# Splitting one opening load over two hardware queues and re-ordering the first quarter of a fused attention and SwiGLU kernel

## The chip, the cores and the metric

The kernel runs on one core of a Trainium2 chip. The metric is device microseconds (us) of that core; the median of five runs of the kernel before is 332.36 us (331.88 to 332.77). The core's engines are PE (TensorE, matrix products into eight PSUM banks), DVE (VectorE), ACT (ScalarE), POOL (GpSimd) and SP (SyncE). Each takes its own instructions strictly in program order. POOL here does nothing but issue loads; SP issues the transposes done by DMA and the stores.

## The reference

Causal sliding-window attention, window 64, over 8 batches of 8 heads of 576 tokens with 64 channels, and then a gated feed-forward block (FFN) on the 4608 tokens:

```python
scores = (1/8) * q @ k.T;  allowed where 0 <= i - j < 64
attn = softmax(scores);  x = attn @ v           # [4608, 512] over all heads
g = x @ w_gate;  val = x @ w_val                # [4608, 1536]
out = (g * sigmoid(g) * val) @ w_out            # [4608, 512]
```

All inputs and the output are float32 in memory; the matrix products run in bfloat16.

## The kernel before

**Tiles.** Attention works on 36 blocks of 128 tokens (n = 0 to 35). The FFN works on nine chunks of 512 tokens, four blocks each, and on twelve pieces f of 128 hidden channels. Tokens cross batches at 4.5 blocks, so blocks 4 and 13 (and others) need two loads for each of q, k and v.

**Two regimes.** The opening covers the attention of blocks 0 to 13 and FFN chunks 0 and 1. It is written out by hand as two strings of short words, `LOADS` (L162) and `STEPS` (L166), which `build` (L675) reads word by word; each word appends its operations to the engines' queues in that order. After it a regular loop (from L717) runs the FFN of chunks 2 to 8, with the second FFN product of the chunk before and the attention of the blocks ahead between its pieces. `_Graph` (L31) derives the semaphore waits from what each operation reads and writes.

**The words of `LOADS`.** Each issues DMAs, nearly all from POOL's queue: `q:n`, `kq:n`, `v:n` load a block (`kq` is two DMAs, q first, 128 KB in bfloat16 each), `w:a:b` loads pieces a to b-1 of w_gate and then of w_val (two DMAs), `wo:a:b` loads pieces of w_out in one DMA. `ld:n` in `STEPS` loads q, k and v of block n. `f:0` is `first_load` (L285): k of block 0 in float32, in two halves of 64 partitions, which are not cast by the DMA but by the words `ca` and `cd`. `init` builds the identity and the masks on DVE.

**The words of `STEPS`.** `warm:a:b` is a products of b columns that nobody reads, and `W:a` is a such products of 512 columns. `TQ:n`, `TK:n` transpose q and k on PE (4 instructions into one bank); `qa`, `ka` evict the result on ACT and `qd`, `kd` on DVE. `T:0:h` with `ea`/`ed` does the same for the first k. `TD:n` transposes k and q by two DMAs on SP's queue. `S:n` is the 24 score products and two exponentials on ACT; `M:n` masks the result on DVE (two operations). A block that had `B:n` before its scores has the mask added by two PE products of 512 columns and needs no `M`. `A0:n` and `A1:n` are the two phases of the product with v (16 instructions each; the second waits for the end of the first), `N:n` is its normalisation on DVE (four operations). `X:n` transposes the result on PE, evicted by `xa` or `xd`; `XD:n` does it with a DMA. `F:c:f:t0:t1` is piece f of FFN chunk c for the token columns t0 to t1 (0 to 512 if not given): four products with w_gate, the tanh on ACT, four products with w_val. `U` does the two DVE operations (L611, L613) of the oldest `F` that has not had its own yet, and frees its two banks. `O:c:u` is the product with w_out for 128 tokens: 12 products of 512 columns and a store.

**What orders it.** An operation that needs a bank takes the one freed longest ago in program order and waits until it has been emptied, so PE can run ahead of DVE only by the banks that are left. An `F` over columns t0 to t1 waits only for the blocks of x in that range. The first `F` of the kernel before, `F:0:7:0:256`, needs blocks 0 and 1 and stands behind `X:2`.

Of the kernel before, what the change touches and what calls it, by code (L numbers as in the profile page):

```python
# [7 lines left out]
B, H, S, D = 8, 8, 576, 64  # L8
DM, DFF = H * D, 1536
T = B * S  # L10
# [139 lines left out]
class _Kernel:  # L150
# [9 lines left out]
    LAST = NFC  # L160
    NI = 1
    LOADS = """  # L162
    f:0 init q:0 kq:1 kq:2 v:1 v:0 kq:3 v:2 v:3 w:7:9 w:1:2 w:5:6 kq:4 kq:5 w:3:4 w:4:5 w:6:7 v:5 w:2:3 v:6
    v:4 w:9:10 w:0:1 kq:6 v:7 kq:7 w:10:12
    """
    STEPS = """  # L166
    warm:45:64 B:0 B:1 ca:0:0 cd:0:1 T:0:1 T:0:0 ea:0:1 TQ:0 ld:8 wo:0:6 ed:0:0 qa:0 W:1 TQ:1 S:0 qd:1 TK:1
    ld:9 kd:1 W:1 TQ:2 S:1 qd:2 TK:2 kd:2 W:2 S:2 W:1 A0:0 A0:1 A1:0 A1:1 ld:10 N:0 TQ:3 B:3 qa:3 N:1 TK:3 X:0
    ka:3 xa:0 M:2 W:1 S:3 X:1 A0:2 xd:1 A1:2 ld:11 N:2 W:1 A0:3 A1:3 N:3 W:1 X:2 F:0:7:0:256 xd:2 U X:3
    F:0:8:0:384 xd:3 F:0:1 U U F:0:5 U TK:4 TQ:4 ld:12 ka:4 TQ:5 F:0:7:256:512 qd:4 TK:5 qa:5 F:0:8:384:512 U  # L170
    S:4 U F:0:3 kd:5 M:4 S:5 U F:0:4 M:5 U F:0:6 U F:0:2 U A0:4 A0:5 A1:4 ld:13 wo:6:12 A1:5 F:0:9 N:4 N:5 X:4
    F:0:0 U xa:4 X:5 U TK:6 xa:5 TQ:6 ld:14 F:1:0:0:128 ka:6 U F:1:1:0:256 qa:6 TQ:7 U F:1:2:0:256 qd:7 S:6
    TK:7 U F:1:3:0:256 kd:7 F:0:10 M:6 U U A0:6 S:7 A1:6 ld:15 TQ:8 TK:8 N:6 F:0:11 M:7 ka:8 qd:8 X:6 A0:7
    xa:6 S:8 U A1:7 ld:16 F:1:4:0:384 N:7 F:1:5:0:384 U X:7 U TQ:9 xa:7 F:1:6:0:384 M:8 qa:9 TK:9 U F:1:7 kd:9
    TD:10 U A0:8 S:9 A1:8 ld:17 F:1:8 N:8 M:9 X:8 TQ:11 xa:8 F:1:9 U qd:11 A0:9 TK:11 U A1:9 ka:11 F:1:10 N:9
    TK:12 U X:9 ka:12 TQ:12 F:1:11 xd:9 qd:12 TD:13 S:10 U S:12 F:1:0:128:512 M:10 F:1:1:256:512 M:12 A0:10 U
    S:11 A1:10 U F:1:2:256:512 F:1:3:256:512 N:10 F:1:4:384:512 U XD:10 F:1:5:384:512 O:0:0 U U U M:11 O:0:1
    A0:11 S:13 A1:11 O:0:2 N:11 M:13 X:11 O:0:3 xd:11 F:1:6:384:512 U TD:14 TD:15
    """

    def __init__(self, nc, q, k, v, wg, wv, wo, out):
# [103 lines left out]
    def first_load(self, n):  # L285
        (_, b, s, L), = self.segs(128 * n, 128)
        for u in range(2):
            d = self.ff[n][64 * u:64 * u + 64].rearrange("p h j d -> p h (j d)")
            a = self.k[b, 4 * u:4 * u + 4, s:s + L, :].rearrange("h (p j) d -> p h (j d)", j=2)
            self.g.op("sp", lambda e, d=d, a=a: e.dma_start(d, a), writes=[("ff", n, u)], dma=True)  # L290

    def cast(self, n, half, eng):
        hs = slice(2 * half, 2 * half + 2)
# [489 lines left out]
```

The softmax here doesn't subtract the row's maximum and nothing guards it: scores larger than these inputs give would overflow.

## Time and profile before

| what | value |
|---|---|
| median of five runs | 332.36 us (331.88 to 332.77) |
| the profiled execution, its own time | 332.36 us, of it 330.2 us span |
| first `F` begins on PE | 17.55 us |
| first `O` begins on PE | 71.48 us |
| regular loop begins (`F` of chunk 2) | 83.27 us |
| POOL busy issuing loads | without a pause from 1.25 to about 68 us |
| DMA engines | 9 tenths or more in each slice up to about 200 us |

Times in the profile are counted from the start of the span. A row of the timeline gives start and length, the engine, the line, what was written from what, and how many instructions were merged; a length includes the time to drain, so the distance between starts is what an instruction occupies its engine. "POOLq", "SPq" and "ACTq" are the queues on which DMAs are issued; "to landing" is counted from the start of the issue. The granted TensorE clock is 1.00 throughout in this profile.

### The profile page before, as it was taken

Reading aid. Unit: us, or ns where it says so; the run is one execution under the profiler, and the core shown is the slowest. Engines: PE = TensorE matmul, PEld = TensorE weight load, DVE = VectorE, ACT = ScalarE, POOL = GpSimd, SP = SyncE. Lnnn points to the kernel's source line nnn. Section 1 sums busy time; section 2 is a strip of 40 time slices with the busy share of each in tenths; the row PEclk is TensorE's granted clock in tenths of the full one; section 3 lists DMA queues with packets and bytes.
Section 4 is the critical chain, followed back from the end, with each engine's and each line's share of the span. In section 5 each row is a group of like instructions: output and inputs, shape, how many; then the busy total and the mean of one; then the engine's idle time right before and its main releaser. Section 6 shows DMA issues by size and latency. Waiting matters only on the chain.

```text
span 330.2 us, 8380 instructions
## 1 busy us (share of the span) xinstructions
PE 324.8 (98%) x3543; PEld 166.3 (50%) x3543; DVE 216.7 (66%) x457; ACT 136.0 (41%) x247; POOL 116.5 (35%) x145
## 2 busy tenths in 40 slices
PE   7999999999999999999999999999999999999996
PEld 5565665564455444444445454545454544444444
DVE  5689999992467748585757676767676766555520
ACT  3736566453344334343525252525343432332222
POOL 8999999957017506060706060100000000000000
PEclk9999999999999999999999999999999999999999
DMA  9999999999999999999999999542424111100012
GB/s 102 168 169 172 154 183 155 158 144 185 185 172 137 165 179 75 181 85 172 85 173 82 174 70 189 66 112 36 126 35 128 34 64 34 64 34 32 32 64 98
DMA packets 169366, 38.56 MB, mean 117 GB/s; under 512 B 160369, under 2 KB 164849, under 8 KB 169329
## 3 DMA queue, kind: packets, MB, share of 16 engines
q0 software_dynamic: 123600, 18.75, 86.3%
q1 hardware_dynamic: 45584, 19.21, 29.3%
q8 instruction: 28, 0.46, 0.6%
q14 instruction: 10, 0.07, 0.1%
q10 hardware_dynamic: 144, 0.07, 0.1%
HBM read 37.75 MB, written 9.44 MB: 143 GB/s over the span
## 4 chain that ended last, share of the span: by engine, by line
PE 93%; DVE 3%; DMA 2%; SPq 0%; issue 0%
PE ps L602 55%; PE ps L635 27%; PE ps L421 3%; DMA xT<-xb 2%; PE ps L534 2%; PE ps L309 2%; PE ps L471 2%; PE ps L665 1%; PE ps L568 1%; PE ps L401 1%; PE ps L357 1%; DVE xb L493 1%; DVE xb L556 0%; SPq L584 0%; DVE mask L267 0%
## 5 line engine op out<-in xcount | busy, mean ns | idle before, releaser
L611 DVE SCALAR_TENSOR_TENSOR uu<-sig,ps 128x512 bf16<-128x512 bf16 (+3 forms) x117 | 75.2, 643 | 66.5 <-ACT sig L608 66.2
L602 PE MATMUL ps<-xT,Wg 128*128 128x512 bf16 (+3 forms) x468 | 112.5, 363 | 0.4 <-DMA xT<-xb 0.4
L602 PE MATMUL ps<-xT,Wv 128*128 128x512 bf16 (+3 forms) x468 | 112.5, 363 | 0.0
L608 ACT ACTIVATE sig<-ps 128x512 bf16<-128x512 f32 (+3 forms) x117 | 66.0, 565 | 89.3 <-PE ps L602 89.2
L635 PE MATMUL ps<-Wo,hT 128*128 128x512 bf16 x420 | 97.8, 379 | 0.0
L613 DVE SCALAR_TENSOR_TENSOR hT<-uu,ps 128x512 bf16<-128x512 bf16 (+3 forms) x117 | 75.5, 645 | 4.0
L371 POOL DMA_DIRECT2D va<-in_v_dram x40 | 39.5, 1021 | 87.9 <-PE ps L534 86.6
L602 PEld LDWEIGHTS ps<-xT,Wv 128*128 128x128 bf16 x468 | 45.0, 98 | 48.9 <-DVE hT L613 0.5
L602 PEld LDWEIGHTS ps<-xT,Wg 128*128 128x128 bf16 x468 | 43.8, 98 | 46.5 <-DMA xT<-xb 1.1
L635 PEld LDWEIGHTS ps<-Wo,hT 128*128 128x128 bf16 x420 | 39.9, 98 | 46.6
L431 ACT ACTIVATE pt<-ps 128x512 bf16<-128x512 f32 x72 | 37.8, 600 | 26.8 <-PE ps L421 26.7
L647 ACT ACTIVATE ost<-ps 128x512 f32<-128x512 f32 x35 | 20.9, 597 | 66.1 <-PE ps L635 66.0
L283 POOL DMA_DIRECT2D qn<-in_q_dram x40 | 40.5, 1032 | 3.2 <-issue 2.4
L283 POOL DMA_DIRECT2D kn<-in_k_dram x39 | 39.7, 1041 | 1.4 <-DMA kn<-in_k_dram 1.3
L437 DVE TENSOR_TENSOR pt<-pt,mask 128x512 bf16<-128x512 bf16 x66 | 24.3, 417 | 0.2
L556 DVE TENSOR_TENSOR xb<-ps,rp 128x448 bf16<-128x448 f32 (+1 forms) x36 | 18.5, 514 | 1.2
L553 DVE RECIPROCAL rp<-ps 128x7 f32<-128x7 f32 (+1 forms) x36 | 6.7, 187 | 15.5 <-PE ps L534 15.5
L421 PE MATMUL ps<-qT,kT 64*64 64x64 bf16 (+1 forms) x864 | 16.0, 205 | 0.2
L421 PEld LDWEIGHTS ps<-qT,kT 64*64 64x64 bf16 x864 | 12.4, 109 | 7.2 <-DVE hT L613 4.2
L534 PE MATMUL ps<-va,pt 64*64 64x65 bf16 x728 | 11.5, 193 | 0.1
L493 DVE TENSOR_TENSOR xb<-ps,rc 128x256 bf16<-128x256 f32 x24 | 10.2, 424 | 0.8
L377 POOL DMA_DIRECT2D Wv<-in_moe_w_val_dram x10 | 9.7, 969 | 0.0
(50 smaller groups left out, 104.9 us busy)
## 6 DMA issues: line engine op xcount, KB each, us to landing
out_dram<-ost SPq DMA_DIRECT2D x35, 256.0 KB, 2.5
qn<-in_q_dram POOLq DMA_DIRECT2D x32, 128.0 KB, 7.6
va<-in_v_dram POOLq DMA_DIRECT2D x32, 128.0 KB, 6.7
kn<-in_k_dram POOLq DMA_DIRECT2D x31, 128.0 KB, 7.9
Wo<-in_moe_w_out_dram POOLq DMA_DIRECT2D x2, 768.0 KB, 12.2
Wg<-in_moe_w_gate_dram POOLq DMA_DIRECT2D x8, 128.0 KB, 5.4
Wv<-in_moe_w_val_dram POOLq DMA_DIRECT2D x8, 128.0 KB, 5.3
Wg<-in_moe_w_gate_dram POOLq DMA_DIRECT2D x2, 256.0 KB, 5.6
```

The costliest lines, as they stand in the source:

```text
L283: self.g.op("pool", lambda e, d=d, a=a: e.dma_start(d, a), writes=ks, dma=True)
L371: g.op("pool", lambda e, d=d, a=a: e.dma_start(d, a), writes=ks, dma=True)
L421: r = e.matmul(sv[h][o:o + 64, c, q0:q1], self.kT[ps, c, kk:kk + 64], qT[ps, c, q0:q1], start=not biased, stop=not biased or c == 3 and kk ...
L431: g.op("act", lambda e, po=po, si=si: e.activation(po, si, ACTF.Exp, scale=SCALE), reads=[bk], writes=[pk])
L437: "dve", lambda e: e.tensor_tensor(po, po, m, ALU.mult), reads=[pk, "mask"], writes=[pk]))
L556: g.op("dve", lambda e, xo=xo, rb=rb, a=a: e.tensor_tensor(xo, a[:, :, 0:64], rb, ALU.mult), reads=[bk] + rk, writes=wk)
L602: r = e.matmul(bank[:, 0:n], W[:, kk, f * 128:f * 128 + 128], xT[:, kk, t0:t1], start=(kk == 0), stop=(kk == NK - 1))
L608: g.op("act", lambda e: e.activation(sig[:, 0:n], G[:, 0:n], ACTF.Tanh, scale=0.5), reads=[gk], writes=[("sig", i)])
L611: g.op("dve", lambda e: e.scalar_tensor_tensor(uu[:, 0:n], sig[:, 0:n], 1.0, G[:, 0:n], ALU.add, ALU.mult), reads=[("sig", i), gk], writes ...
L613: g.op("dve", lambda e: e.scalar_tensor_tensor(hT[:, f, t0:t1], uu[:, 0:n], 0.5, V[:, 0:n], ALU.mult, ALU.mult), reads=[("uu", i), vk], wr ...
L635: r = e.matmul(OB[:, :], hT[:, f, 128 * u:128 * u + 128], self.Wo[:, f, :], start=(f == 0), stop=(f == NF - 1))
L647: g.op("act", lambda e: e.activation(ost[:, :], OB[:, :], ACTF.Copy), reads=[ok], writes=[("ost", io)])
```

## The change

The two halves of k of block 0 are issued from SP and from ACT, one each, instead of both from SP. The order of loads and of steps in the opening is replaced as a whole. Names that differ: the warm-up is 50 products of 86 columns; `B:1` stands behind `TQ:0`; v of block 0 is loaded ahead of v of block 1; the first weights are pieces 2, 3 and then 0, 1, in 256 KB DMAs; the weights come in 16 DMAs instead of 20; both halves of w_out are loaded behind block 12; the first `F` is `F:0:2:0:128`, behind `X:1`, and pieces 2, 3, 0 and 1 of chunk 0 are cut in the token direction, as are pieces 0 to 4 of chunk 1 (128 and 384 columns). Block 4 gets `B:4` and loses `M:4`; `X:5` becomes `XD:5`; blocks 12 and 13 change places between `TD` and PE transposes. The loop is not touched.

```diff
     LOADS = """
-    f:0 init q:0 kq:1 kq:2 v:1 v:0 kq:3 v:2 v:3 w:7:9 w:1:2 w:5:6 kq:4 kq:5 w:3:4 w:4:5 w:6:7 v:5 w:2:3 v:6
-    v:4 w:9:10 w:0:1 kq:6 v:7 kq:7 w:10:12
+    f:0 init q:0 kq:1 kq:2 v:0 kq:3 v:1 v:2 w:2:4 v:3 w:0:2 kq:4 kq:5 kq:7 kq:6 w:5:6 w:6:7 w:7:9 v:6 v:4
+    w:9:10 v:7 v:5 w:4:5 w:10:12
     """
     STEPS = """
-    warm:45:64 B:0 B:1 ca:0:0 cd:0:1 T:0:1 T:0:0 ea:0:1 TQ:0 ld:8 wo:0:6 ed:0:0 qa:0 W:1 TQ:1 S:0 qd:1 TK:1
-    ld:9 kd:1 W:1 TQ:2 S:1 qd:2 TK:2 kd:2 W:2 S:2 W:1 A0:0 A0:1 A1:0 A1:1 ld:10 N:0 TQ:3 B:3 qa:3 N:1 TK:3 X:0
-    ka:3 xa:0 M:2 W:1 S:3 X:1 A0:2 xd:1 A1:2 ld:11 N:2 W:1 A0:3 A1:3 N:3 W:1 X:2 F:0:7:0:256 xd:2 U X:3
-    F:0:8:0:384 xd:3 F:0:1 U U F:0:5 U TK:4 TQ:4 ld:12 ka:4 TQ:5 F:0:7:256:512 qd:4 TK:5 qa:5 F:0:8:384:512 U
-    S:4 U F:0:3 kd:5 M:4 S:5 U F:0:4 M:5 U F:0:6 U F:0:2 U A0:4 A0:5 A1:4 ld:13 wo:6:12 A1:5 F:0:9 N:4 N:5 X:4
-    F:0:0 U xa:4 X:5 U TK:6 xa:5 TQ:6 ld:14 F:1:0:0:128 ka:6 U F:1:1:0:256 qa:6 TQ:7 U F:1:2:0:256 qd:7 S:6
-    TK:7 U F:1:3:0:256 kd:7 F:0:10 M:6 U U A0:6 S:7 A1:6 ld:15 TQ:8 TK:8 N:6 F:0:11 M:7 ka:8 qd:8 X:6 A0:7
-    xa:6 S:8 U A1:7 ld:16 F:1:4:0:384 N:7 F:1:5:0:384 U X:7 U TQ:9 xa:7 F:1:6:0:384 M:8 qa:9 TK:9 U F:1:7 kd:9
-    TD:10 U A0:8 S:9 A1:8 ld:17 F:1:8 N:8 M:9 X:8 TQ:11 xa:8 F:1:9 U qd:11 A0:9 TK:11 U A1:9 ka:11 F:1:10 N:9
-    TK:12 U X:9 ka:12 TQ:12 F:1:11 xd:9 qd:12 TD:13 S:10 U S:12 F:1:0:128:512 M:10 F:1:1:256:512 M:12 A0:10 U
-    S:11 A1:10 U F:1:2:256:512 F:1:3:256:512 N:10 F:1:4:384:512 U XD:10 F:1:5:384:512 O:0:0 U U U M:11 O:0:1
-    A0:11 S:13 A1:11 O:0:2 N:11 M:13 X:11 O:0:3 xd:11 F:1:6:384:512 U TD:14 TD:15
+    warm:50:86 B:0 ca:0:0 cd:0:1 T:0:0 T:0:1 ea:0:0 ed:0:1 TQ:0 ld:8 B:1 qa:0 TQ:1 S:0 qd:1 TK:1 ld:9 kd:1 W:1
+    TQ:2 S:1 qd:2 TK:2 kd:2 W:1 A0:0 S:2 A1:0 N:0 TQ:3 B:3 qa:3 M:2 W:1 X:0 xa:0 TK:3 ka:3 W:1 A0:1 W:1 S:3
+    A1:1 ld:10 N:1 A0:2 A1:2 ld:11 N:2 W:2 X:1 F:0:2:0:128 xa:1 U X:2 F:0:3:0:256 xd:2 A0:3 U A1:3
+    F:0:2:128:384 N:3 F:0:0:0:384 U X:3 U TQ:4 xa:3 F:0:1:0:384 qd:4 TK:4 ld:12 wo:6:12 wo:0:6 U TQ:5 ka:4
+    F:0:3:256:512 qd:5 TK:5 F:0:0:384:512 U TQ:7 ka:5 F:0:1:384:512 U F:0:2:384:512 U TK:7 qa:7 S:5 U B:4 kd:7
+    S:4 TQ:6 TK:6 M:5 kd:6 F:0:5 qd:6 U S:6 S:7 F:0:6 M:6 F:0:7 M:7 U F:0:8 U U A0:4 A1:4 ld:13 F:0:9 N:4 U
+    A0:5 A0:6 A0:7 A1:5 ld:14 A1:6 ld:15 A1:7 X:4 N:5 xa:4 F:0:4 N:6 XD:5 F:0:10 N:7 U X:6 X:7 xa:6 F:0:11 U
+    xa:7 U TQ:8 TK:8 ld:16 qa:8 F:1:0:0:128 F:1:1:0:128 U F:1:2:0:128 F:1:3:0:128 U TQ:9 U ka:8 F:1:4:0:128 U
+    TK:9 qa:9 S:8 U F:1:5 kd:9 M:8 U A0:8 TD:10 S:9 A1:8 ld:17 F:1:6 N:8 M:9 X:8 TQ:11 xa:8 F:1:7 U qd:11 A0:9
+    A1:9 U F:1:8 N:9 TK:11 F:1:9 U TD:12 kd:11 X:9 F:1:10 U xd:9 F:1:11 U U F:1:0:128:512 S:10 U F:1:1:128:512
+    M:10 F:1:2:128:512 U A0:10 U S:11 A1:10 F:1:3:128:512 N:10 F:1:4:128:512 U XD:10 M:11 O:0:0 U A0:11 S:12
+    A1:11 TK:13 N:11 TQ:13 O:0:1 M:12 kd:13 qd:13 X:11 S:13 xd:11 O:0:2 M:13 O:0:3 TD:14 TD:15
     """
...
     def first_load(self, n):
...
-            self.g.op("sp", lambda e, d=d, a=a: e.dma_start(d, a), writes=[("ff", n, u)], dma=True)
+            self.g.op(("sp", "act")[u], lambda e, d=d, a=a: e.dma_start(d, a), writes=[("ff", n, u)], dma=True)
```

## The prediction

> **What bounds the kernel now.** First the page's busy shares and its chain:
>
> ```profile
> PE 324.8 (98%) x3543; PEld 166.3 (50%) x3543; DVE 216.7 (66%) x457; ACT 136.0 (41%) x247; POOL 116.5 (35%) x145
> ...
> PE 93%; DVE 3%; DMA 2%; SPq 0%; issue 0%
> ```
>
> PE sets the end. Only the opening is touched, so I next read busy time by stretch (length, then PE, PEld, DVE, ACT, POOL with instruction counts):
>
> ```profile
> 17.30:71.50 54.20, 54.12 (x778) 33.32 (x778) 49.34 (x117) 31.26 (x63) 52.59 (x65) 1.00 2.01 163
> 71.50:83.05 11.55, 11.55 (x116) 5.66 (x114) 4.97 (x16) 3.05 (x7) 6.99 (x8) 1.00 1.99 174
> ```
>
> From the first `F` PE is full, with DVE close behind (91%). What the change can win lies before 17.55, or in less PE work and fewer small gaps behind it. Then the timeline of the first stage, with the chain through it:
>
> ```profile
> 1.02 2.58 PE L345 MATMUL ps<-wz 128*128 128x64 bf16 x45 [1.02 <-DVE wz L255]
> 4.33 1.89 PE L401 MATMUL ps<-nmask,ident 128*128 128x512 bf16 x4 [0.73 <-DVE nmask L268]
> 5.69 0.42 ACT L299 ACTIVATE cc<-ff 128x256 bf16<-128x256 f32 x1 [3.46 <-DMA ff<-in_k_dram]
> 6.45 0.63 PE L309 MATMUL ps<-ident,qn 128*128 128x128 bf16 x4
> 7.87 0.64 PE L421 MATMUL ps<-qT,kT 64*64 64x128 bf16 x24
> 9.56 0.44 PE L421 MATMUL ps<-qT,kT 64*64 64x128 bf16 x24
> 11.55 0.86 PE L471 MATMUL ps<-va,pt 64*64 64x65 bf16 x56
> 12.30 0.18 DVE L490 RECIPROCAL rc<-ps 128x4 f32<-128x4 f32 x1 [1.50 <-PE ps L471]
> 17.55 0.60 PE L602 MATMUL ps<-xT,Wg 128*128 128x256 bf16 x4
> 20.05 1.03 PE L602 MATMUL ps<-xT,Wg 128*128 128x512 bf16 x4
> ```
>
> The reader sees k cast at 5.69, q transposed at 6.45, first scores at 7.87, first product with v at 11.55 (held by v), normalisation from 12.30, FFN from 17.55. Last, POOL and its landings, one issue at a time:
>
> ```profile
> 5.74 1.78 POOL L371 DMA_DIRECT2D va<-in_v_dram  x2
> ...
> 10.93 0.84 POOL L377 DMA_DIRECT2D Wg<-in_moe_w_gate_dram  x1
> ...
> va<-in_v_dram POOLq DMA_DIRECT2D x1, 128.0 KB, 4.7
> Wv<-in_moe_w_val_dram POOLq DMA_DIRECT2D x1, 256.0 KB, 5.7
> ```
>
> A load of q, k or v takes POOL 0.87 us and lands 4.7 to 5.0 us after its start (5.5 around 18 to 25); weights take 0.73 and land after 5.1 to 6.8.
>
> **k in halves.** Both came from SP: starts 0.73 and 1.53, landing 2.8 and 4.1 later, at 3.5 and 5.6. From ACT the second starts at about 0.74 and lands between 3.5 and 4.8, so casts (0.42) end by 5.2. But `B:0` comes first on PE: 45 products of 64 columns took 2.58 less 0.18 of drain, 53 ns each; 50 of 86 take 72 ns each, to 4.60, and two mask products at the 0.43 between the L401 starts end at 5.46. Transposes of k start there instead of at 6.04. The next step, `TQ:0`, needs q, issued at 1.25 with 5.0 to land: 6.25, against 6.45. Halves alone are worth 0.15 to 0.2. The issue on ACT (0.60 to 0.74) stands ahead of its table load (0.74 to 2.02), hidden by ACT's 3.46 idle before 5.69; uncovered it would cost 0.74. On SP nothing is queued behind the pair until the DMA transposes at 54.6.
>
> The Trainium skill ("Trainium Kernel Development and Optimization", Key Constraints) speaks against more: DMAs from SP, ACT and POOL share 16 engines, and a second queue saves only issue time. By that rule the second half gains the 0.8 between the starts, landing near 4.8; by the rows' better bound 3.5. Either way `B:0` hides it.
>
> **PE's pace.** 512 columns were 0.43 apart at 4.33 and 0.216 in the `O` rows (12 in 2.59); full pace begins near 9.05. PE idled 0.73 between warm-up and masks, and full pace came 4.7 after it went on at 4.33. The longer warm-up closes that pause, so counted from 1.02 it comes at 5.7. I take that, being nearest the row; the other bound is 9.05 as before, no gain.
>
> The skill ("TensorE: Matmul & The Clock Gate", Part 1) has half rate released after one busy window of about 3.4 us whose phase is free. By it the release could come anywhere from 4.4 to 7.9. That supports the early pace but makes it vary.
>
> **To the end of block 3.** At the early pace: `TQ:0` 6.33, evicted 7.35; `S:0` 7.5 behind `B:1` and `TQ:1` (7.87 before); `TK:1` 7.98 (k landed 7.95); `S:1` 9.1 (9.56); `TK:2` 9.65; `kd:2` to 10.45. v of block 0, issued at 5.74 instead of 6.6, lands at 10.45: `A0:0` 10.5 (11.55). `S:2` stands between the phases: `N:0` 11.4 to 12.5 (12.30 before). `X:0` 12.6, `xa:0` (0.6) behind `qa:3` to 13.5, `ka:3` to 14.1, `S:3` 14.25. `A1:1` is queued behind `S:3` on PE, and `N:1` waits for it: 15.0 to 16.1, though v of block 1 landed at 13.1. Here half the gain is lost. `X:1` 16.25, first `F` 16.45 (w_val of pieces 2, 3, issued behind ten loads and w_gate at 10.85, lands at 10.85 + 5.7 = 16.55, just in time for its second half). `N:2` to 17.2, `X:2` 17.3, `F:0:3` 17.7 behind `xa:1`, `A:3` 18.6, `F:0:2:128:384` 19.2, `F:0:0:0:384` 20.05 (its w_val, three issues later: 13.2 + 6.8, the longest landing of a weight there, = 20.0), `X:3` 21.4, done at 21.6.
>
> At 21.6 chunk 0's attention is finished and 3.48 us of FFN done (a whole `F` is 1.73; 128, 256, 256 and 384 columns). Before, the same attention was finished and 2.17 done at 20.05; 1.31 more makes 21.36. **Balance here: +0.24** despite the earlier first `F`, because block 3 comes after it. At the old pace `S:0` falls to 8.05 and all of this comes 0.55 later: +0.8.
>
> **From there to the loop.** FFN, transposes and `O` are equal to a few hundredths on PE: 128-column products are 56 ns apart, a quarter of 0.216. On top come `B:4`, two of 0.216, +0.43; `X:5` gone, -0.22. Attention is interleaved otherwise. Rows price it: a phase pair with scores between costs 0.74, scores alone 0.47, a pair alone 0.72 (15.30 to 15.95 and the start), two pairs together 0.91. Before: three lone scores, a double (0.72), two pairs, six mixed ones (0.69 to 0.85): 7.57. After: four lone scores, a double, `A:4` and `A:9` alone, `A:5` to `A:7` together (1.3), three mixed: 8.06, +0.49. Sum of added PE work **+0.70**.
>
> Against it stands DVE. `M:4` leaves 0.75; ten cuts instead of nine add 0.3 (two operations of 0.28 per 128 columns against 0.69 per 512). DVE stays at nine tenths, and its place matters more than its sum. The normalisations of blocks 4 to 7 come in one knot: I get DVE without a pause from 38.7, with 33.6 of work to 72.3, while PE needs 31.3. Five 128-column pieces then meet banks that DVE has not emptied (about 0.5), and `X:8` waits for `N:8` (about 0.35). The before had 0.52 of such gaps (0.23 before the `F` at 46.12, 0.13 at 40.16, 0.16 at 69.55). Bounds for the after: none to 1.6; I take 0.7, nearest the two named waits with some covered. Net **+0.18**.
>
> Loads: four fewer weight DMAs make `ld:8` start at 35.1 instead of 37.5. Each `F` has 0.6 to 1 us in hand (pieces 7, 8: 25.9 + 6.8 = 32.7 against 33.3). w_out, 768 KB, took 9.8 and 14.6; issued at 48 it is there by 65, needed near 71: nothing, and 0.5 us for each 0.5 later than 71 if not. `XD:5`, issued near 42.0, takes 6.5 to 8.2 by the transposes' rows: 48.5 to 50.2, needed at 49.25 by `F:1:5`; 0 to 1.0, taken as 0 because 7.1 (the `XD` at 71.1) makes 49.1. What TD words queue on SP behind it has over 5 us. The loop is unchanged; its one wait, 0.38 for x at 117.64, may shift by 0.4 either way.
>
> Sum: 0.24 + 0.70 + 0.18 = +1.1. The profiled execution is itself the median, 332.36 (span 330.2 and 2.16 around it): **333.5 us**.
>
> **Rivals.**
>
> Faster: v-first pays in full. For it: `A0:0` is 1.05 earlier, and v held this very row. If `S:3` does not hold `A1:1` (x of block 0 and k of block 3 evicted by 13.4 rather than 14.1), block 3's attention ends at 20.5, -0.86 instead of +0.24; with the added 0.70 and no more gaps than before's less 0.5 that DVE's relief could cover, 332.36 - 0.86 + 0.70 - 0.5 = 331.7. Against: three ACT evictions of 0.6 stand in line. It decides if the first `F` starts before 16.0.
>
> Nothing: the early pace holds, the new gaps equal the old, and the 0.49 for lone phases, a difference of two sums of a dozen rows each, is not there: 332.36 + 0.24 + 0.43 - 0.22 = 332.8, within the margin. For it: where a transpose filled such a pair (60.05 to 60.87) little was lost. Against: `A:4` and `A:9` have nothing between their phases.
>
> Slower still: a late transfer. `XD:5` at 8.2 plus the old pace: 333.5 + 1.0 + 0.55 = 335.0. For it: DMA engines at nine tenths, landings of up to 10 us from 40 on. Against: SP's rows stayed at 6.5 to 8.2 even then.
>
> The halves do nothing: k lands late from a shared queue, but PE reaches it at 5.46. Only later than 5.4 it costs, 0.2; inside the forecast.
>
> **How the numbers follow.** Forecast (slower by 0.66 to 1.8) 0.42; slower still 0.12; nothing 0.20; faster 0.26. A measurement of this kernel tells about 0.2%, 0.66 us, from no change. Range: down to 331.6 for the faster case, up to 334.7: forecast plus the old pace (0.55) and part of the late transfer. The forecast's own range is 333.0 to 334.2. Chances: faster 0.26, same 0.20, slower 0.54.
>
> **What would show it.** Right: k transposed near 5.5, `TQ:0` near 6.3, `A0:0` near 10.5, `N:1` about 15.0, first `F` near 16.5, block 3's `X` after 21, more PE idle with DVE as releaser between 45 and 55, loop start near 84.4. Wrong: first `F` before 16.0, loop start before 83.27, or a PE wait for weights.

## The result and the profile after

The changed kernel takes 333.79 us (median of 24 runs, 332.82 to 336.56), the kernel before 332.28 us (45 runs on the same chips). The ratio is 1.0044, with a 95% interval of 1.0032 to 1.0055: **slower by 1.46 us** (1.06 to 1.83), small but clear of the 0.2% that a measurement tells. The forecast was 333.5, slower by 1.1, in a range of 331.6 to 334.7. The profiled execution of the changed kernel took 333.53 us, 331.7 of it span. In 4 of its 25 executions (the 24 and the profiled one) the mean granted TensorE clock was 0.995 instead of 1.00, and these took 334.44 to 336.56 us; the other 21 have a median of 333.60, 1.32 above the kernel before.

The page of the changed kernel, busy shares and the chain by engine:

```profile
PE 324.8 (98%) x3553; PEld 166.3 (50%) x3553; DVE 216.9 (65%) x457; ACT 135.7 (41%) x247; POOL 113.5 (34%) x141
...
PE 95%; DMA 2%; POOL 2%; issue 1%; DVE 0%; ACT 0%; POOLq 0%
```

PE is exactly as busy as before (324.8 us) in a span 1.5 us longer. The chain now has an "issue" share of 1%, time in which PE waited for nothing that the profile shows, and POOL and a load of q: it leaves PE in the first 13 us. PE's timeline of the changed kernel there (start, length, line, what it wrote from what, and in brackets the idle time before it and what ended it):

```profile
1.02 3.77 PE L345 MATMUL ps<-wz 128*128 128x86 bf16 x50 [1.02 <-DVE wz L255]
5.43 0.63 PE L309 MATMUL ps<-ident,cc 128*128 128x128 bf16 x4
5.86 0.63 PE L309 MATMUL ps<-ident,qn 128*128 128x128 bf16 x4
6.29 0.83 PE L401 MATMUL ps<-nmask,ident 128*128 128x512 bf16 x2
6.96 0.39 PE L309 MATMUL ps<-ident,qn 128*128 128x128 bf16 x4
7.27 0.45 PE L421 MATMUL ps<-qT,kT 64*64 64x128 bf16 x24
10.25 0.22 PE L471 MATMUL ps<-va,pt 64*64 64x65 bf16 x4 [0.48 <-ACT pt L431]
12.17 0.38 PE L309 MATMUL ps<-ident,qn 128*128 128x128 bf16 x4 [1.22 <-DMA qn<-in_q_dram]
13.04 0.39 PE L568 MATMUL ps<-ident,xb 128*128 128x128 bf16 x4
16.72 0.39 PE L602 MATMUL ps<-xT,Wg 128*128 128x128 bf16 x4
20.48 0.33 PE L602 MATMUL ps<-xT,Wg 128*128 128x384 bf16 x1
21.41 0.66 PE L602 MATMUL ps<-xT,Wg 128*128 128x384 bf16 x3 [0.60 <-issue]
22.55 0.39 PE L568 MATMUL ps<-ident,xb 128*128 128x128 bf16 x4
```

The start is earlier, as forecast: first scores 7.27 (7.87 before), first product with v 10.25 (11.55), first `F` 16.72 (17.55). Then the lead is lost. q of block 3 holds PE 1.22 us at 12.17, with block 0's finished result queued behind it until 13.04. At 20.48 PE does one product of a group of four and stands still before the second: in this program a group waits for semaphores only ahead of its first product. The second starts 0.93 us after the first, where products of 384 columns are otherwise 0.16 apart, so the stop takes 0.77, more than the 0.60 that the row calls idle. Block 3 is transposed at 22.55.

| from the profiles, us | before | forecast | after |
|---|---|---|---|
| first transposes of k | 6.04 | 5.46 | 5.43 |
| first product with v | 11.55 | 10.5 | 10.25 |
| first `F` | 17.55 | 16.45 | 16.72 |
| attention of chunk 0 done, with 3.48 of FFN | 21.36 | 21.6 | 22.78 |
| first `O` | 71.48 | not given | 72.97 |
| loop begins | 83.27 | 84.4 | 85.23 |
| end of span | 330.2 | 331.3 | 331.7 |

So 1.42 us are lost up to the end of block 3's attention (22.78 less 21.36), 0.54 from there to the loop (62.45 against 61.91), and 0.46 come back in the loop (246.47 against 246.93): together 1.50. Most of what comes back is one wait of the kernel before, here among PE's waits from 84 us on. The changed kernel has none of that length there: the DMA transpose in question landed 1.4 us later than before (119.03 against 117.60), and PE came 1.9 later.

```profile
PE ps L602 <- DMA xT<-xb: 0.4, 1, 0.4
```

### The profile page after: what moved, and what is told of

It is laid out like the page before. It is cut to its first block, busy times and chain, and to the rows that moved or that the text cites. A ratio compares the mean times of both kernels' runs of the same rounds, so it can differ in the third digit from the quotient of the medians.

```text
span 331.7 us, 8397 instructions
## 1 busy us (share of the span) xinstructions
PE 324.8 (98%) x3553; PEld 166.3 (50%) x3553; DVE 216.9 (65%) x457; ACT 135.7 (41%) x247; POOL 113.5 (34%) x141
## 4 chain that ended last, share of the span: by engine, by line
PE 95%; DMA 2%; POOL 2%; issue 1%; DVE 0%; ACT 0%; POOLq 0%
PE ps L602 57%; PE ps L635 28%; PE ps L421 3%; PE ps L534 2%; DMA qn<-in_q_dram 2%; PE ps L471 1%; PE ps L309 1%; POOL qn L283 1%; PE ps L568 1%; PE ps L665 1%; POOL kn L283 1%; PE ps L401 0%; DVE xb L493 0%; POOL va L371 0%; ACT xT L299 0%
## 5 line engine op out<-in xcount | busy, mean ns | idle before, releaser
L371 POOL DMA_DIRECT2D va<-in_v_dram x40 | 38.6, 1005 | 91.0 <-PE ps L534 87.6
L283 POOL DMA_DIRECT2D qn<-in_q_dram x40 | 39.4, 1002 | 4.9 <-PE ps L421 4.1
L283 POOL DMA_DIRECT2D kn<-in_k_dram x39 | 38.1, 997 | 1.1 <-PE ps L602 1.1
L534 PEld LDWEIGHTS ps<-va,pt 64*64 64x64 bf16 x728 | 9.4, 108 | 0.6 <-DVE hT L613 0.4
```

Source lines behind the costliest of these rows:

```text
L283: self.g.op("pool", lambda e, d=d, a=a: e.dma_start(d, a), writes=ks, dma=True)
L371: g.op("pool", lambda e, d=d, a=a: e.dma_start(d, a), writes=ks, dma=True)
L534: r = e.matmul(bb[b][0][ws, 65 * sl:65 * sl + 65], self.pt[(n + j) % self.NP][ks, h, ws], vv[ks, h, 0:65], start=m == q[0], stop=m == q[-1])
```

## The experiments

Twelve kernels were run. "Ratio" is to the kernel before in the same job, with its 95% interval.

**k alone.** The edit in the kernel before:

```diff
-            self.g.op("sp", lambda e, d=d, a=a: e.dma_start(d, a), writes=[("ff", n, u)], dma=True)
+            self.g.op(("sp", "act")[u], lambda e, d=d, a=a: e.dma_start(d, a), writes=[("ff", n, u)], dma=True)
```

> The kernel before, with nothing but the second half of k moved to ACT's queue. My theory: PE reaches the transposes of k only after its four mask products (4.33 to 6.05 in the trace of before), so an earlier k hides there; k lands near 4.3, the first transposes still start at 6.0, and the time stays within 0.2 us of before (332.3). Rival, k is what the opening waits for: the first transposes start near 5.5 and the time falls by 0.4 to 0.6 us. Second rival, a further queue disturbs the loads: slower by 0.3 or more.

Ratio 0.9996 (0.9981 to 1.0010); the first transposes of k start at 6.00 (6.04 before). k is not what that opening waits for, and no loss from a second queue shows. The profiled execution shows something else, on PE's timeline:

```profile
12.89 0.87 PE L471 MATMUL ps<-va,pt 64*64 64x65 bf16 x56 [1.43 <-DMA va<-in_v_dram]
18.90 0.60 PE L602 MATMUL ps<-xT,Wg 128*128 128x256 bf16 x4
```

v of block 0 came 1.3 us later than in the profile of before, with nothing moved that touches it, and the first `F` 1.35 later; the loop began at 84.64. The span was still only 331.0: loads vary by a microsecond between executions, and single profiles have to be read with that.

**k back on one queue**, in the changed kernel (the edit above reversed).

> The changed kernel with both halves of k on SP's queue again. My theory: with the masks of block 1 moved behind the first q, k does set the first transposes (5.43 in the trace after); they fall back to about 6.0 and everything up to the first product with v, which v holds at 10.2, has room for most of it: 0 to 0.3 us slower than the changed kernel, 333.8 to 334.1. Rival, the second queue is what costs the 1.5 us: back to about 332.5.

Ratio 1.0052 (1.0034 to 1.0070), not to be told from the changed kernel's 1.0044. The transposes of k start at 5.82 instead of 5.43, the first product with v at 10.36 instead of 10.25. The halves gain 0.4 us where they act, and 0.1 is left of it one load later. The second queue is not the loss.

**What a wait can do to PE's clock.** In the profiled execution of `both_on_sp` the granted clock falls to 0.50 from 12.33 to 15.74 us: two mask products of 512 columns stand 0.43 apart at 12.43, as in the first microseconds, where the changed kernel has 0.22. PE had been busy 1.78 of the 3.41 us before. The profiles of three kernels further down show the same, each time for 3.4 us or twice that: `transposes_a` (0.50 from 68.37 to 71.78, after a wait of 1.89), `x_first` (11.90 to 18.73, after one of 3.12) and `transposes_b` (76.53 to 83.35, within one of 7.12). Not every wait brings it: 1.43 us in `halves_only` and 1.53 in `mask_4` did not. The start of the changed kernel is more open to it, since PE is busy 2.35 of the 4 us from 8.00 on, 3.91 before. A mean clock of 0.995 over 331 us is one such stretch (an estimate from 3.4 us at half clock: 1.7 us of PE's work). Counted at a clock of 1.00 alone, the medians are 333.60 for the changed kernel and 333.63 for `both_on_sp`.

**The mask of block 4 back on DVE**, in the changed kernel:

```diff
-    S:5 U B:4 kd:7 S:4 TQ:6 TK:6 M:5 kd:6
+    S:5 U kd:7 S:4 TQ:6 TK:6 M:5 M:4 kd:6
```

> The changed kernel without the two mask products of block 4 on PE; block 4's mask goes back to DVE (two operations, 0.75 us). My theory, added PE work counts in full because PE sets the pace there: 0.43 us faster than the changed kernel, 333.3. Rival, DVE is the bound between 38 and 50 us: no gain, or up to 0.4 us slower than the changed kernel.

Ratio 1.0069 (1.0042 to 1.0097): no gain. But the profile was not fit to tell PE from DVE, for a stop lay in the way, again inside a group of four:

```profile
28.23 0.23 PE L309 MATMUL ps<-ident,qn 128*128 128x128 bf16 x1
29.99 0.33 PE L309 MATMUL ps<-ident,qn 128*128 128x128 bf16 x3 [1.53 <-issue]
```

**The stops.** Counting the products that PE had begun at each stop gives 348 and 721 in the changed kernel (0.60 and 0.16 us idle), 473 and 721 in `both_on_sp` (1.01 and 0.33), 473 in `mask_4` (1.53). The distances are 125 and 248. The number of the product stays, whatever stands there in the program. (At 473 of `both_on_sp` a new group begins, and the profile puts the wait down to ACT; the changed kernel passes the same place, 0.38 us after the same scores, without waiting.) The pages also list an instruction queue: 28 packets, 0.46 MB, so some 16 KB each. PE begins 3553 products and 3553 weight loads; 28 blocks of 124 such pairs are 3472 of the 3553, so one packet for every such block fits its share of the queue. In the stretch from 18 to 24 us of the changed kernel one of them is seen, begun at 19.1:

```profile
q8 instruction: 1, 0.02, 0.9%
```

This suggests that PE waits for its own program, whose blocks come over the DMA engines. The start of each packet can be set beside the moment at which PE goes on:

| kernel, products begun | packet begins | PE goes on | between |
|---|---|---|---|
| changed, 348 | 19.11 | 21.41, after the stop | 2.30 |
| changed, 721 | 43.88 | 46.10, after the stop | 2.22 |
| `both_on_sp`, 473 | 28.05 | 30.64, after the stop | 2.59 |
| `mask_4`, 473 | 27.71 | 29.99, after the stop | 2.28 |
| before, 348 | 17.20 | 21.99, no stop | 4.79 |
| changed, 473 | 25.40 | 29.02, no stop | 3.62 |

PE goes on 2.2 to 2.6 us after the packet began; where it arrives later than that, it does not stop. Two kernels test it. First the limits are moved in the changed kernel, by a warm-up of equal time in fewer products:

```diff
-    warm:50:86
+    warm:34:128
```

> The changed kernel with a warm-up of 34 products of 128 columns instead of 50 of 86: the same time on PE (34 x 107 ns = 3.6 us), 16 products and 16 weight loads fewer in PE's program. In the trace after, PE stands still at 20.5 to 21.4 and at 45.8 to 46.1 in the middle of a group of four products, where no semaphore can hold it, 373 products apart, and the trace has one packet of 16 KB on an instruction queue at 19.1 and 43.9. My theory, PE waits for its own instructions there: the stops move by 16 products to other places and shrink or go, 0.3 to 0.9 us faster than the changed kernel (332.9 to 333.5). Rival, the stop at 20.5 is w_gate or the vector engine: it stays at the same product with the same 0.6 us, time unchanged.

Ratio 1.0030 (1.0017 to 1.0044); median 333.62. The profile has no stop at 348, 473 or 721 any more. One is left, where weight load 846 is next, 125 behind 721, 2.29 us after its packet began:

```profile
52.29 0.25 PE L471 MATMUL ps<-va,pt 64*64 64x65 bf16 x7 [0.32 <-issue]
```

Block 3 is transposed at 21.68 (22.55), the loop begins at 84.62 (85.23), the span is 331.1 (331.7). The direction is as expected, but the intervals of the two ratios overlap; the difference, 0.14% or 0.46 us, is not secured by the times. At a clock of 1.00 alone nothing is left of it: the medians are 333.59 and 333.60, and the profiled execution of `warm_34` was the fastest of its twelve. So the cause was put into the other kernel:

```diff
-        a = self.wz[:, :].unsqueeze(1).to_broadcast([128, 4, 128])
+        a = self.wz[:, :]
...
-            for _ in range(count):
-                r = e.matmul(bank[:, :], self.wz[:, :], a, start=True, stop=True)
+            for _ in range(4 * count):
+                r = e.matmul(bank[:, 0:128], self.wz[:, :], a, start=True, stop=True)
```

> The kernel before, with each fill product of 512 columns (W) replaced by four of 128: the same columns and nearly the same PE time, 24 more products in PE's program ahead of the first F. In the traces so far PE stood still in the middle of a group only at its products number 348, 473, 721 and 846, which lie 124 or 125 apart (with their weight loads and waits 256 instructions, 16 KB), and only where PE had used up the 124 before in some 6 us or less. My theory, PE waits there for its own instructions: with 24 more products, number 348 is reached near 17.7 instead of 22 us, hardly 4 us after number 224, so a stop of 0.5 to 2 us shows near number 348 and the time rises by 0.4 to 1.5 us over before (332.7 to 333.8). Rival, the stops come from late loads or from banks: no stop there, within 0.2 us of before.

Ratio 1.0022 (1.0012 to 1.0031), slower by 0.73 us, as expected, and on PE's timeline:

```profile
17.64 0.60 PE L602 MATMUL ps<-xT,Wg 128*128 128x256 bf16 x4
18.07 0.27 PE L602 MATMUL ps<-xT,Wv 128*128 128x256 bf16 x1
19.34 0.49 PE L602 MATMUL ps<-xT,Wv 128*128 128x256 bf16 x3 [0.99 <-issue]
```

At 18.9 us, in the stop, PE had begun 348 products; the packet had begun at 16.99, 2.35 us before PE went on. Up to there the execution is level with the kernel before (first `F` 17.64 against 17.55); the kernel before passes number 349 near 22 us, amid whole pieces, without a stop. The loop begins 0.71 us later (83.98 against 83.27), close to the 0.73 of the times, and all twelve executions were at a clock of 1.00. So PE stops at this place when it arrives there too soon after the packet began. That the packet is what it waits for follows from the size, the count and these times together; no row says it. The bound of some 6 us for 124 products, in the expectation above, does not hold: the 124 before product 473 took 7.4 us in `both_on_sp`, which stopped, and the 124 before 348 took 5.65 in `both_on_sp` and `mask_4`, which did not.

**PE work or DVE work.** With the limits out of the way, the two added terms of the forecast were each taken out of `warm_34`: the mask of block 4 (the edit of `mask_4`), and the pauses between phases:

```diff
-    S:6 S:7 F:0:6 M:6 F:0:7 M:7 U F:0:8 U U A0:4 A1:4 ld:13 F:0:9 N:4 U
+    S:6 F:0:6 M:6 F:0:7 U F:0:8 U U A0:4 S:7 A1:4 ld:13 F:0:9 N:4 M:7 U
...
-    A0:9 A1:9 U F:1:8 N:9 TK:11 F:1:9
+    A0:9 TK:11 A1:9 U F:1:8 N:9 F:1:9
```

> warm_34 with block 4's mask on DVE again instead of two mask products on PE. With the warm-up of 34 products the 124-product limits lie where PE is slow to reach them, so this compares PE work with DVE work alone. My theory: 0.3 to 0.45 us faster than warm_34 (333.62), 333.2 to 333.3, first O 0.4 earlier than its 72.42 if the same loads come equally late. Rival, DVE is the bound: no gain or slower than warm_34 by up to 0.4.

> warm_34 with work put between the phases of the product with v that had nothing between them: the scores of block 7 between those of block 4, the transposes of k of block 11 between those of block 9. My theory, that arrangement was worth 0.49 of the predicted loss: 0.3 to 0.5 us faster than warm_34, 333.1 to 333.3; in the trace block 4's pair with scores takes about 0.74 and the lone double of scores before F:0:6 shrinks from 0.72 to 0.47. Rival, the lone phases cost nothing because DVE and ACT need that pause: same time as warm_34.

Ratios 1.0040 (1.0028 to 1.0052) and 1.0039 (1.0026 to 1.0051); neither is faster than `warm_34`: PE work taken out there did not shorten the time. In `phases_filled` PE gets its scores for less and then waits for DVE, in the very place that was relieved (block 7's mask comes later, and block 4 to 7's normalisations with it):

```profile
39.25 0.74 PE L471 MATMUL ps<-va,pt 64*64 64x65 bf16 x64 [0.19 <-DVE pt L437]
40.80 0.81 PE L602 MATMUL ps<-xT,Wg 128*128 128x512 bf16 x3 [0.48 <-DVE rc L490]
```

(Of the second row's four products one is missing in the trace; the weight loads put the first at 40.57, so that wait is nearer 0.3.) From block 3's transpose to the first `O` it takes 51.24 us, `warm_34` 50.74. In `mask_4_shifted` PE's waits are for loads instead. The w_gate of piece 5 landed at 29.52, 28.39 in `warm_34`:

```profile
29.87 0.81 PE L602 MATMUL ps<-xT,Wg 128*128 128x512 bf16 x3 [0.48 <-DMA Wg<-in_moe_w_gate_dram]
```

Its same stretch takes 50.59. The condition of the comparison, loads that come equally late, was not met; whether DVE would have taken back the 0.43 of the mask is not shown.

**The wait for q of block 3**, in the changed kernel:

```diff
-    N:0 TQ:3 B:3 qa:3 M:2 W:1 X:0 xa:0 TK:3
+    N:0 W:1 X:0 xa:0 TQ:3 B:3 qa:3 M:2 TK:3
```

> The changed kernel with the transpose of block 0's result put ahead of the transposes of q of block 3 on PE. In the trace after, q of block 3 landed at 12.0 (5.4 us after its issue) and held PE 1.22 us, with the finished block 0 queued behind it until 13.04. My theory, this wait is carried into chunk 0: the result's transpose starts near 12.3, k of block 3 is evicted near 14.0 instead of 14.5, 0.2 to 0.5 us faster than the changed kernel (333.3 to 333.6). Rival, scores of block 3 wait for k and q of block 3 anyway: no change.

Ratio 1.0064 (1.0034 to 1.0094), no gain; at a clock of 1.00 the median is 333.49 (five executions), against 333.60. Block 3's scores need its q and k whatever is transposed before them, so the likely reason is the rival's; the profile cannot show it, because v of block 0 landed 2.4 us later there than in the changed kernel and held PE for 3.12 us, with the half clock behind it.

**The early start on the kernel before.** A first form, `v0_first`, with the same loads and the steps in nearly the same order, had the load of block 10 ahead of the products that read its slot: block 1 was multiplied with v of block 10 and waited for it.

> The kernel before, with the start of the changed one and nothing else of it: k in halves on two queues, the warm-up of 50 products of 86 columns, block 1's masks behind the first q, v of block 0 loaded ahead of v of block 1, the scores of block 2 between the phases of block 0's product with v, block 0 transposed before q of block 3. The first FFN pieces and all that follows stay as before. My theory, the early start is worth something and the loss lies in what follows: first F at 17.0 to 17.3 instead of 17.55, held there by its weights (11.7 + 5.7 = 17.4 for the second half), 0.2 to 0.5 us faster than before (331.8 to 332.1). Rival, the early start itself is no gain because loads set it: within 0.1 us of before. Rival, the start is where the change loses: slower than before by 0.5 or more.

Its 376.21 us (ratio 1.133) tell nothing of the start. The second form:

```diff
-    f:0 init q:0 kq:1 kq:2 v:1 v:0 kq:3
+    f:0 init q:0 kq:1 kq:2 v:0 v:1 kq:3
...
-    kd:2 W:2 S:2 W:1 A0:0 A0:1 A1:0 A1:1 ld:10 N:0 TQ:3 B:3 qa:3 N:1 TK:3 X:0 ka:3 xa:0 M:2 W:1 S:3 X:1 A0:2 xd:1 A1:2
+    kd:2 W:1 A0:0 S:2 A1:0 N:0 A0:1 A1:1 ld:10 M:2 X:0 xa:0 N:1 TQ:3 B:3 qa:3 TK:3 ka:3 W:1 X:1 xd:1 A0:2 S:3 A1:2
```

with the halves, the warm-up and the steps up to `TK:1` of the changed kernel.

> The kernel before with the start of the changed one and the rest as before: v0_first with the load of block 10 behind the products that read the slot it fills. My theory, the early start is worth something and the loss lies in what follows: first F at 17.0 to 17.3 instead of 17.55, held by its weights (11.7 + 5.7 = 17.4 for the second half), 0.2 to 0.5 us faster than before (331.8 to 332.1). Rival, the early start is no gain because loads set it: within 0.1 us of before. Rival, the start is where the change loses: slower than before by 0.5 or more.

Ratio 1.0029 (1.0010 to 1.0047), runs from 331.58 to 334.89. In the profiled execution:

```profile
10.80 0.23 PE L471 MATMUL ps<-va,pt 64*64 64x65 bf16 x4 [1.20 <-DMA va<-in_v_dram]
16.64 0.72 PE L471 MATMUL ps<-va,pt 64*64 64x65 bf16 x32 [0.71 <-ACT pt L431]
17.73 0.49 PE L602 MATMUL ps<-xT,Wg 128*128 128x256 bf16 x3
```

The first scores came at 6.43 (7.87 before), the first product with v at 10.80 (11.55), held by its load, and the first `F` at 17.73, where it was before. What held PE last ahead of it were ACT's exponentials of block 3, at 16.64; w_val landed at 17.75, before the second half needed it at 18.17. An early start is not kept. The spread of 3.3 us goes with the clock: six executions at 1.00 have a median of 332.23 (331.58 to 332.81), within 0.1 us of before as the first rival has it, and six at 0.990 to 0.995 took 332.99 to 334.89.

**A version to beat both.** Work taken off PE, DVE and ACT together should count, so transposes of the kernel before were given to DMA: q and k of block 11 (`transposes_a`), and the results of blocks 8 and 9 as well (`transposes_b`).

```diff
-    TD:10 U A0:8 ... X:8 TQ:11 xa:8 F:1:9 U qd:11 A0:9 TK:11 U A1:9 ka:11 F:1:10 N:9 TK:12 U X:9 ka:12 TQ:12 F:1:11 xd:9
+    TD:10 TD:11 U A0:8 ... X:8 xa:8 F:1:9 U A0:9 TK:12 U A1:9 ka:12 F:1:10 N:9 U X:9 TQ:12 F:1:11 xd:9
```

In `transposes_b`, `X:8 xa:8` and `X:9 xd:9` become `XD:8` and `XD:9` in these lines too.

> The kernel before with q and k of block 11 transposed by two DMAs on SP's queue (behind those of block 10) instead of on PE, and k of block 12 in the pause of block 9's product with v that k of block 11 filled. PE loses 8 products (0.44 us) and DVE and ACT an eviction each (0.35 and 0.6). My theory: where PE and DVE are both full, only work taken from both moves the time; 0.3 to 0.5 us faster than before (331.7 to 331.9). q and k of block 11 landed at 54.4, the DMAs need till about 66, the scores stand at 68.2. Rival, as in mask_4_shifted and phases_filled, removed PE work comes back as waits on DVE: within 0.15 us of before. Rival, two more DMA transposes are late: PE waits for kT or qT near 68, slower.

> transposes_a with the results of blocks 8 and 9 also transposed by DMA (XD for X): 8 more products off PE (0.44 us), one eviction off ACT and one off DVE; chunk 2 needs them only at 83. My theory: another 0.3 to 0.5 us faster, 331.2 to 331.6, and so faster than both kernels. Rival, waits on DVE take it back: as transposes_a. Rival, four more DMA transposes make the later ones late (block 13's scores near 76, chunk 2 at 83): slower than transposes_a by 0.5 or more.

Ratios 1.0076 (1.0053 to 1.0098) and 1.0264 (1.0237 to 1.0290): both slower. `transposes_a` and then `transposes_b`, PE's waits, and from the DMA issues of `transposes_b` the second half of w_out:

```profile
67.44 0.45 PE L421 MATMUL ps<-qT,kT 64*64 64x128 bf16 x24 [1.89 <-DMA kT<-kn]
```

```profile
79.63 2.72 PE L635 MATMUL ps<-Wo,hT 128*128 128x512 bf16 x6 [7.12 <-DMA Wo<-in_moe_w_out_dram]
```

```profile
Wo<-in_moe_w_out_dram POOLq DMA_DIRECT2D x1, 768.0 KB, 24.1
```

w_out took 14.6 us to land before, 19.4 in `transposes_a`, 24.1 here, and PE stood 7.12 us for it. In both kernels the wait brought the half clock as well: behind it the six products of the row above took 2.72 us, where twelve take 2.59 at full clock. No version tried beats the kernel before.

## Why the prediction was right, and where it was not

The direction and the size within a third held, and one reason: the lead of the first `F` is real but small, and it is spent before block 3 is through. The parts did not: forecast +0.24, +0.88 and nothing for the three stretches, measured in the profiles +1.42, +0.54 and -0.46. That their sum came near was in good part luck. By its steps:

- **k in halves.** Right. Forecast 5.46 for the first transposes, measured 5.43; worth nothing in the kernel before (`halves_only`), 0.1 at the first product with v in the changed one. The halves landed at 4.2 and 3.7, the second nearer the bound from the rows (3.5) than that of the issue time alone (4.8), and the masks hid which. ACT's table load moved from 0.74 to 1.49, hidden as forecast.
- **PE's pace.** Early, as forecast, but a microsecond later than the 5.7 taken: the two products at 6.29 take 0.67 to the next start, one slow and one fast, so full pace came near 6.7 (9.05 before). The Trainium skill ("TensorE: Matmul & The Clock Gate", Part 1) has the phase of the release free; the runs agree, in that the same 50 products took 3.35 us in `mask_4` and 3.77 in the changed kernel.
- **To the end of block 3.** Forecast +0.24, measured +1.42: the step that was mis-sized most. Two things were missing in it. q of block 3 took 5.4 us to land where the row said 4.8, which brought block 0's transpose from 12.6 to 13.04 (though the time of `x_first` suggests that this alone decides nothing). And PE stopped at product 348, which took 0.77. The trace of before holds no such stop, so no row could price it. The remaining 0.4 are not divided further.
- **From there to the loop.** Forecast +0.88, measured +0.54, but not by its terms. The 0.43 of `B:4` and the 0.49 of the lone phases were in the program (the sum of 8.06 counts five lone scores, as the order of steps has; the text says four), yet taking them out gained nothing; and the two waits for DVE that made the 0.7 of gaps did not come. These lines of PE's timeline of the changed kernel are halves of the first two of the five short pieces that were to wait, and `X:8`:

```profile
47.64 0.39 PE L602 MATMUL ps<-xT,Wv 128*128 128x128 bf16 x4
47.87 0.39 PE L602 MATMUL ps<-xT,Wg 128*128 128x128 bf16 x4
54.97 0.39 PE L568 MATMUL ps<-ident,xb 128*128 128x128 bf16 x4
```

  The pieces follow one another 0.22 apart, without a wait. From 38.7 to 72.3 DVE was busy 31.46 of 33.60 us and PE 33.37, so the knot of normalisations was there without holding PE; the one stop in this stretch, at product 721, took 0.3 and was no term. In `phases_filled` what was taken from PE was waited for at DVE; that this holds of the mask too is not shown. Adding PE work and DVE gaps as independent terms was wrong here, and the sum was near because the errors had opposite signs.
- **Loads.** PE waited for no weights, as forecast; `XD:5` landed 7.0 us after its issue, taken as 7.1. Landings were longer than the rows (w_val of pieces 0 and 1: 8.1, forecast 6.8; the second half of w_out 21.4, before 14.6), still in time; w_val of pieces 0 and 1 only because PE had stopped, for it landed at 21.28 and would have been needed near 21.1.
- **The loop.** Its one wait went away, 0.38 of the 0.4 that were allowed either way.

Of the rivals, "faster" fell by its own test: the first `F` came at 16.72, not before 16.0. "Nothing" (332.8) falls with the interval, whose lower end is 1.06. "The halves do nothing" is true of the kernel before. Of the signs named, the idle of PE with DVE as its releaser between 45 and 55 did not show. How the 1.46 us divide between the stops in the program, the half clock in some executions and the order of the opening is open: moving the limits gave 0.46 with overlapping intervals, and nothing at a clock of 1.00.

## What to carry to other kernels

Where two engines and the DMA are all nine tenths full, a term taken from one of them is not yet a gain; try the edit alone, and look for the wait that takes its place. An earlier start counts only if nothing behind it waits for a load or another engine. Count instructions as well as time: many short products in a row can use up the program faster than it arrives. Before comparing small differences, look at the granted clock of each execution: a wait can cost more than its length.

## What was not expected of the hardware

PE stops at fixed counts of its own instructions (products 348, 473, 721 and 846, 0.16 to 1.53 us idle) when it gets there less than about 2.2 us after the packet on the instruction queue began, and goes on 2.2 to 2.6 us after that start; the packets began 13 to 94 products ahead of these places, and where PE needs longer for those, as with whole pieces, it passes without a stop. Where it happens inside a group no dependence explains it, and the profile calls it "issue". What starts a packet is open.

PE's granted clock can fall to 0.50 for 3.4 us, or twice that, after much shorter waits: in `both_on_sp` the longest wait ahead of it was 1.11 us, and PE had been busy half of the 3.41 us before.

Landings of one and the same load vary between executions: v of block 0, issued near 6.6, landed at 11.3 in the profile of before and at 12.8 in that of `halves_only`.

DMA transposes and a load in flight seem to cost each other time: with two more of them issued just behind it, one 768 KB load landed after 19.4 us instead of 14.6, with four more after 24.1, one execution each.
